# Softmax denominators from two partial sums: four key chunks added on GpSimd, two on VectorE, joined by the ones matmuls of TensorE

## The chip, the cores and the metric

The kernel runs on one core of one Trainium2 chip. Times are device microseconds (us) of one execution, so smaller is better. TensorE (PE in the profile; PEld is its weight load), VectorE (DVE), ScalarE (ACT), GpSimd (POOL) and SyncE (SP) are its engines. The program gives each its own instruction list, and the views of the profile name which engine waited for which.

## The reference, cut to what matters

```python
# q, k, v: (4, 8, 768, 64); 16 clusters for each head
q_assign = argmax(einsum('bhsd,hcd->bhsc', q_n, c_n), -1)      # the same for k
mask = q_assign[:, :, :, None] == k_assign[:, :, None, :]
scores = where(mask, scale * q @ k.T, -1e9)
attn = exp(scores - max(scores));  attn = attn / (sum(attn, -1) + 1e-9)
x = (attn @ v)                     # then, for each of 3072 rows of 512:
# a gate picks 2 of 8 rank-16 adapters; out = x + sum of w * (x @ A[e]) @ B[e]
```

The change touches only `sum(attn, -1)`, the denominator of the softmax.

## The kernel before

Two heads form a pair; there are 16 pairs, four for each batch element. A pair's 768 queries are worked off in three thirds of 256, and its 768 keys in six chunks of 128, which lie on the partitions. For each third, TensorE computes the scores, ScalarE takes exp of two chunks at a time into the tile `ET` (keys on partitions, 2 heads x 256 queries in the free dimension), and TensorE multiplies with `v`. The value matmuls of a third are issued three thirds behind its scores. The denominator needs the sum of the six chunks, and then the sum over the 128 partitions, which TensorE does with a matrix of ones:

```python
def add_unit(p, t, u, ready):                     # u: which two chunks have just been through exp
    f = lambda k_: ET[p, t][:, k_].rearrange("p h c -> p (h c)")
    def reduce():                                 # chunks 3, 4, 5 and T, which is GpSimd's sum of 0, 1, 2
        nc.vector.tensor_reduce(SS[p][:, :, t * TQ:(t + 1) * TQ]...,
                                ET[p, t][:, 3:T + 1].rearrange("p k h c -> p h c k"), axis=AX.X, op=ALU.add)
    if u < 2:
        W.op("POOL", 1.3, lambda: nc.gpsimd.tensor_tensor(f(T), f(T if u else 0), f(u + 1), ALU.add), ...)
    else:
        W.after([("add", p, t, 1)], lambda x: W.op("DVE", 2.2, reduce, ...))

def denominators(p):                              # once a pair: "the denominator group"
    ps = misc([128, 384])
    for h in range(2):
        for f in range(2):
            o = 32 * (2 * h + f)
            nc.tensor.matmul(ps[o:o + 32, :], ones[:, 0:32], SS[p][:, h, f * 384:(f + 1) * 384])
    # ... VectorE: transpose, reciprocal, transpose; DMAs spread the result to all rows (rDb)
```

Two more parts play a role. `route(p)` is a group of four TensorE matmuls of the same shape, whose input is the q and k of a later pair, turned by VectorE (`nc.vector.transpose` into `qkT`). And the last pair has a wider form, `denominators_wide`, in two parts.

`W` is a small simulator that runs while the program is built; it only decides in which order the instructions are put into each engine's list. Numbers such as 1.3 and 2.2 in it are its guesses of durations.

The softmax here doesn't subtract the row's maximum and nothing guards it: scores larger than these inputs give would overflow.

## Time and profile before

| kernel before | |
|---|---|
| time, median of 4 runs | 364.99 us (364.70 to 365.08) |
| the profiled execution | 367.25 us, a span of 365.5 on the core |
| TensorE, VectorE, ScalarE, GpSimd busy | 88%, 81%, 56%, 50% |
| TensorE and VectorE busy from 100 to 300 us, of 200 | 187.2 and 182.1 us |
| granted TensorE clock | 0.963 in the profiled execution |

The profiled execution is 2 us slower than the median of the timed runs. Among all 33 runs of this kernel the times lie between 364.5 and 368.0. In the 29 of them with a listed clock it lies between 0.961 and 0.972. So a difference of two single profiles is good to some 3 us only; times are compared by their runs.

The costliest groups that matter here: line, engine, operation, out<-in, shapes, count | busy us in total, mean ns of one | idle time of the engine just before them and what ended it.

```profile
L433 DVE TENSOR_REDUCE SS<-ET 128x512 f32<-128x2048 f32 x48 | 182.6, 3804 | 14.7 <-ACT ET L422 9.6
L437 POOL TENSOR_TENSOR ET<-ET 128x512 f32<-128x512 f32 x96 | 122.6, 1277 | 71.7 <-ACT ET L422 68.6
...
L298 DVE STREAM_TRANSPOSE qkT<-qk_pc 128x768 f32<-128x768 f32 x28 | 26.9, 961 | 0.0
L449 PE MATMUL ps<-SS,ones 128*32 128x384 f32 x120 | 22.6, 514 | 3.7 <-DVE SS L433 3.7
```

The reductions alone are 182.6 of VectorE's 296.5 us. A float32 matmul shows as two records, so 120 records are 60 matmuls, four for each of 15 pairs. The view of TensorE's own waits (who waited for whom: total us, how often, longest):

```profile
PE sc L419 <- ACT ET L422: 9.7, 23, 0.7
PE ps L321 <- DVE qkT L298: 7.7, 7, 2.8
...
PE ps L449 <- DVE SS L433: 3.7, 4, 2.3
PE ps L484 <- DVE SS L433: 3.4, 1, 3.4
...
PE ps L321 <- ACT ET L422: 2.2, 2, 1.1
```

L419 are scores, L321 routing, L449 the denominator group, L484 the wide one. This view counts only time in which no matmul is recorded as running; its lines for the start and for the tail's adapter work, which the change leaves as they are, are left out.

```profile
54.01 0.85 PE L321 MATMUL ps<-qkT,cnP 128*32 128x384 f32 x8 [2.83 <-DVE qkT L298]
54.79 4.50 PE L510 MATMUL o_180<-ET,v_nat 128*64 128x256 f32 x24
59.22 0.75 PE L419 MATMUL sc<-Q_1_145,K_1_147 80*128 80x256 f32 x4
59.80 0.64 PE L419 MATMUL sc<-Q_0_144,K_0_146 80*128 80x256 f32 x4
61.17 0.74 PE L419 MATMUL sc<-Q_0_144,K_0_146 80*128 80x256 f32 x4 [0.73 <-ACT ET L422]
61.84 0.83 PE L449 MATMUL ps<-SS,ones 128*32 128x384 f32 x2
65.03 1.43 PE L449 MATMUL ps<-SS,ones 128*32 128x384 f32 x6 [2.35 <-DVE SS L433]
```

The routing group waits 2.83 us for VectorE. Then the 24 records of value matmuls take 4.50 us; elsewhere in this trace the same 24 take 2.81. The denominator group starts at 61.84, stops for the last third's sum, and ends at 66.46: 4.62 us for work that takes 0.85 when its inputs are there. Of the 3.8 us too many, only 2.35 are listed as idle time. The granted clock was halved from 54.9 to 58.3 us and from 65.1 to 68.6, just after each of the two waits (the clock column of the windows view).

### The profile page before, as it was taken

The numbers are of one execution on the slowest core, as the hardware profiler recorded it, in microseconds if no ns is written. First come the engines' busy times: TensorE is split into PE (matmuls) and PEld (weight loads), VectorE is DVE, ScalarE is ACT, GpSimd is POOL, SyncE is SP. The second block draws the span as 40 slices with busy tenths as digits, with TensorE's granted clock in tenths as the row PEclk, the third lists the DMA queues.
The fourth block names the chain that finished last, engine by engine and source line by source line (L and its number), as shares of the span: only waits on it lengthen the run. The fifth ranks groups of instructions, "written<-read, shape, count | busy, mean of one in ns | idle before, by whom it ended". The sixth has DMA issues, their size and how long they took to land.

```text
span 365.5 us, 6465 instructions
## 1 busy us (share of the span) xinstructions
PE 320.4 (88%) x2432; PEld 206.3 (56%) x2444; DVE 296.5 (81%) x324; ACT 204.6 (56%) x233; POOL 184.1 (50%) x211
## 2 busy tenths in 40 slices
PE   4789957899898998898989989898989999996964
PEld 1466544555555565566666655566656557673533
DVE  6328697898989898989798998989897989898052
ACT  3267574374756646658576484665757547471213
POOL 5243737466665645564738347465565464551000
PEclk9758998899999999999999999999999999998999
DMA  7820536154725333535556441717365102020204
GB/s 159 179 43 2 118 72 112 39 87 95 130 72 93 77 64 50 119 56 136 125 124 142 94 75 24 142 30 174 79 164 131 30 12 70 18 82 29 84 4 172
DMA packets 111695, 32.07 MB, mean 88 GB/s; under 512 B 101488, under 2 KB 107504, under 8 KB 111664
## 3 DMA queue, kind: packets, MB, share of 16 engines
q1 hardware_dynamic: 111664, 31.66, 40.3%
q8 instruction: 19, 0.31, 0.4%
q14 instruction: 12, 0.10, 0.1%
HBM read 19.45 MB, written 6.29 MB: 70 GB/s over the span
## 4 chain that ended last, share of the span: by engine, by line
PE 52%; DVE 22%; ACT 8%; issue 6%; SPq 5%; DMA 5%; POOL 0%; DVEq 0%; ACTq 0%
PE o_179 L510 15%; PE o_180 L510 12%; PE sc L419 12%; DVE SS L433 9%; ACT ET L422 7%; PE ps L449 5%; DMA rDb<-rDb 3%; DVE qkT L298 3%; PE ps L321 3%; DVE rDb L460 2%; SPq L472 2%; SPq L154 2%; DVE xT L524 1%; SPq L165 1%; DVE d_t L455 1%
## 5 line engine op out<-in xcount | busy, mean ns | idle before, releaser
L422 ACT ACTIVATE ET<-sc,expbias 128x1024 f32<-128x1024 f32 x144 | 154.5, 1118 | 114.1 <-PE sc L419 113.9
L433 DVE TENSOR_REDUCE SS<-ET 128x512 f32<-128x2048 f32 x48 | 182.6, 3804 | 14.7 <-ACT ET L422 9.6
L437 POOL TENSOR_TENSOR ET<-ET 128x512 f32<-128x512 f32 x96 | 122.6, 1277 | 71.7 <-ACT ET L422 68.6
L510 PE MATMUL o_180<-ET,v_nat 128*64 128x256 f32 x576 | 70.4, 395 | 0.0
L510 PE MATMUL o_179<-ET,v_nat 128*64 128x256 f32 x576 | 68.5, 388 | 0.0
L527 POOL CAST xTb<-xT 128x256 bf16<-128x256 f32 x48 | 18.7, 399 | 81.6 <-DVE xT L524 81.4
L419 PE MATMUL sc<-Q_0_144,K_0_146 80*128 80x256 f32 (+1 forms) x288 | 54.5, 319 | 5.1 <-ACT ET L422 4.6
L419 PE MATMUL sc<-Q_1_145,K_1_147 80*128 80x256 f32 (+1 forms) x288 | 53.3, 309 | 5.7 <-ACT ET L422 5.1
L510 PEld LDWEIGHTS o_180<-ET,v_nat 128*64 128x64 f32 x576 | 40.8, 141 | 27.5 <-issue 6.6
L419 PEld LDWEIGHTS sc<-Q_0_144,K_0_146 80*128 80x128 f32 (+1 forms) x288 | 41.9, 203 | 21.4 <-issue 11.8
L510 PEld LDWEIGHTS o_179<-ET,v_nat 128*64 128x64 f32 x576 | 39.7, 138 | 24.4 <-issue 4.6
L419 PEld LDWEIGHTS sc<-Q_1_145,K_1_147 80*128 80x128 f32 (+1 forms) x288 | 39.6, 190 | 21.6 <-issue 11.1
L298 DVE STREAM_TRANSPOSE qkT<-qk_pc 128x768 f32<-128x768 f32 x28 | 26.9, 961 | 0.0
L449 PE MATMUL ps<-SS,ones 128*32 128x384 f32 x120 | 22.6, 514 | 3.7 <-DVE SS L433 3.7
L321 PE MATMUL ps<-qkT,cnP 128*32 128x384 f32 x128 | 14.3, 518 | 12.2 <-DVE qkT L298 7.7
L274 ACT COPY ot<-ps 128x512 f32<-128x512 f32 x23 | 13.4, 582 | 16.4 <-issue 9.0
L455 DVE STREAM_TRANSPOSE d_t<-ps 128x384 f32<-128x384 f32 x15 | 8.7, 583 | 14.9 <-PE ps L449 14.9
L460 DVE STREAM_TRANSPOSE rDb<-r_pk 128x384 f32<-128x384 f32 x30 | 15.6, 557 | 0.5
L664 PE MATMUL ps<-ident_f,xT 128*128 128x128 f32 x96 | 14.6, 275 | 0.5 <-DVE gt L653 0.4
L449 PEld LDWEIGHTS ps<-SS,ones 128*32 128x32 f32 x120 | 4.3, 108 | 16.4 <-DVE SS L433 10.9
L357 ACT ACTIVATE ohs<-ps,mscale 128x768 f32<-128x768 bf16 x15 | 13.4, 896 | 0.0
L524 DVE TENSOR_TENSOR xT<-o_179,rDb 128x256 f32<-128x256 f32 x24 | 9.6, 400 | 3.1 <-PE o_179 L510 3.1
(151 smaller groups left out, 241.0 us busy)
## 6 DMA issues: line engine op xcount, KB each, us to landing
v_nat<-in_v_dram SPq DMA_DIRECT2D x16, 384.0 KB, 3.8
out_dram<-ot SPq DMA_DIRECT2D x24, 256.0 KB, 2.3
qk_pc<-in_k_dram SPq DMA_DIRECT2D x56, 96.0 KB, 3.5
qk_pc<-in_q_dram SPq DMA_DIRECT2D x56, 96.0 KB, 3.1
rDb<-rDb SPq DMA_DIRECT2D x60, 48.0 KB, 1.9
qk_nat<-in_q_dram SPq DMA_DIRECT2D x4, 192.0 KB, 4.0
qk_nat<-in_k_dram SPq DMA_DIRECT2D x4, 192.0 KB, 4.2
K_1_147<-ohs SPq DMA_DIRECT2D x16, 48.0 KB, 2.1
```

The costliest lines, as they stand in the source:

```text
L274: W.op(eng, n / 1200 + 0.19, lambda: nc.scalar.copy(dst(), src), key=key, then=then)
L298: "DVE", 0.9, lambda: nc.vector.transpose(qkT[p][:, w * S:(w + 1) * S], qk_pc[p][:, w].rearrange("p n d -> p (n d)")),
L321: nc.tensor.matmul(ps[o:o + 32, :].rearrange("p (m c) -> p m c", m=3), cnP[:, j, :], xv[:, w, f])
L419: nc.tensor.matmul(ps[:, i, h, :], kd[0:rows, h, kc * 128:(kc + 1) * 128].bitcast(F32R), qd[0:rows, h, t * TQ:(t + 1) * TQ].bitcast(F32R))
L422: W.op("ACT", 1.12, lambda: nc.scalar.activation(ET[p, t][:, 2 * u:2 * u + 2].rearrange("p a h c -> p (a h c)"), ps[:].rearrange("p a h c ...
L433: nc.vector.tensor_reduce(SS[p][:, :, t * TQ:(t + 1) * TQ].rearrange("p h c -> p h c"), ET[p, t][:, 3:T + 1].rearrange("p k h c -> p h c k ...
L437: W.op("POOL", 1.3, lambda: nc.gpsimd.tensor_tensor(f(T), f(T if u else 0), f(u + 1), ALU.add), ready, key=key)
L449: nc.tensor.matmul(ps[o:o + 32, :], ones[:, 0:32], SS[p][:, h, f * 384:(f + 1) * 384])
L460: nc.vector.transpose(rb[:, f * 384:(f + 1) * 384].rearrange("p (a b) -> p a b", b=32), r_pk[:].unsqueeze(2).to_broadcast([128, 12, 32]))
L510: nc.tensor.matmul(oab[i % 2][64 * h:64 * h + 64, i // 2 % 2, :], v_nat[p][:, h, kc * D:(kc + 1) * D], ET[p, t][:, kc, h, :], start=(kc == ...
L527: "POOL", 0.65, lambda: nc.gpsimd.tensor_copy(xTb[p][:, a:b], xT[p][:, a:b]), y, key=("xb", i))))
L664: nc.tensor.matmul(ps[:, dc * 128:(dc + 1) * 128], xT[NP * b + dc][:, t * 128:(t + 1) * 128], ident_f[:], is_transpose=True, start=(dc == ...
```

## The change

Its intent: take most of the summing from VectorE. GpSimd adds chunks 0 to 3 (three adds in place of two), VectorE adds only chunks 4 and 5 (one two-input add in place of the four-chunk reduction), and the two sums are never added to each other: TensorE multiplies the ones with both and accumulates.

```diff
-            ET[p, t] = etp.tile([128, T + 1, 2, TQ], F32, name="ET")
+            ET[p, t] = etp.tile([128, T, 2, TQ], F32, name="ET")
             if t == 0:
-                SS[p] = wk2.tile([128, 2, S], F32, name="SS")
+                SS[p] = wk2.tile([128, 2, 2, S], F32, name="SS")
...
+        e = lambda k_: ET[p, t][:, k_]
+        a, b = (SS[p][:, i, :, t * TQ:(t + 1) * TQ] for i in range(2))
+        add = lambda x_, k_: W.op("POOL", 1.3, lambda: nc.gpsimd.tensor_tensor(a, x_, e(k_), ALU.add), ready, key=key)
-        if u < 2:
-            W.op("POOL", 1.3, lambda: nc.gpsimd.tensor_tensor(f(T), f(T if u else 0), f(u + 1), ALU.add), ready, key=key)
+        if u == 0:
+            add(e(0), 1)
+        elif u == 1:
+            add(a, 2)
+            add(a, 3)
         else:
-            W.after([("add", p, t, 1)], lambda x: W.op("DVE", 2.2, reduce, max(x, ready), key=("ss", p, t)))
+            W.op("DVE", 0.7, lambda: nc.vector.tensor_tensor(b, e(4), e(5), ALU.add), ready, key=key)
+            W.after([("add", p, t, 1), key], lambda x: W.t.__setitem__(("ss", p, t), x))
...
-        for h in range(2):
-            for f in range(2):
-                o = 32 * (2 * h + f)
-                nc.tensor.matmul(ps[o:o + 32, :], ones[:, 0:32], SS[p][:, h, f * 384:(f + 1) * 384])
+        for i in range(2):
+            for h in range(2):
+                for f in range(2):
+                    o = 32 * (2 * h + f)
+                    nc.tensor.matmul(ps[o:o + 32, :], ones[:, 0:32], SS[p][:, i, h, f * 384:(f + 1) * 384],
+                                     start=(i == 0), stop=(i == 1))
... (the same in denominators_wide)
```

More of the change, by code (lines that the diff above doesn't have):

```diff
@@ L428, in add_unit @@
     def add_unit(p, t, u, ready):
-        f = lambda k_: ET[p, t][:, k_].rearrange("p h c -> p (h c)")
-        def reduce():
-            nc.vector.tensor_reduce(SS[p][:, :, t * TQ:(t + 1) * TQ].rearrange("p h c -> p h c"),
-                                    ET[p, t][:, 3:T + 1].rearrange("p k h c -> p h c k"), axis=AX.X, op=ALU.add)
+        e = lambda k_: ET[p, t][:, k_]
+        a, b = (SS[p][:, i, :, t * TQ:(t + 1) * TQ] for i in range(2))
         key = ("add", p, t, u)
-        if u < 2:
-            W.op("POOL", 1.3, lambda: nc.gpsimd.tensor_tensor(f(T), f(T if u else 0), f(u + 1), ALU.add), ready, key=key)
-        else:
-            W.after([("add", p, t, 1)], lambda x: W.op("DVE", 2.2, reduce, max(x, ready), key=("ss", p, t)))
+        add = lambda x_, k_: W.op("POOL", 1.3, lambda: nc.gpsimd.tensor_tensor(a, x_, e(k_), ALU.add), ready, key=key)
[4 more added lines that the diff above has]
+            add(a, 3)
+        else:
+            W.op("DVE", 0.7, lambda: nc.vector.tensor_tensor(b, e(4), e(5), ALU.add), ready, key=key)
+            W.after([("add", p, t, 1), key], lambda x: W.t.__setitem__(("ss", p, t), x))
     rDb = {}
@@ L482, in denominators_wide @@
         ps = misc([128, n])
-        for h in range(2):
-            nc.tensor.matmul(ps[64 * h:64 * h + 64, :], ones[:], SS[p][:, h, a:a + n])
+        for j in range(2):
+            for h in range(2):
+                nc.tensor.matmul(ps[64 * h:64 * h + 64, :], ones[:], SS[p][:, j, h, a:a + n],
+                                 start=(j == 0), stop=(j == 1))
         def inverse():
```

## The prediction

> **What bounds it now.** The page's busy table: TensorE 320.4 us (88% of 365.5), VectorE 296.5, ScalarE 204.6, GpSimd 184.1. Between 100 and 300 us the windows view shows TensorE busy 37.4 to 38.0 of every 40 us, VectorE 36.2 to 36.6. TensorE sets the pace; VectorE, nearly as full, makes it wait. The waits view, TensorE alone: score matmuls for the exp 9.7 us; routing matmuls for the transposed q/k 7.7; denominator matmuls for the sums 3.7, and once 3.4 at the tail. Another hides in the denominator group: on the chain it takes 1.33 us, but 0.85 where its inputs are there, as the routing group of the same shape (four 128x384 float32 matmuls into four 32-row groups) does: about 5.5 us over the run.
>
> **What the change does.**
> - VectorE: 48 reductions of 3.80 us (182.6) become 48 adds, 128x512 float32. The Trainium skill, "VectorE: DVE Perf Modes", errata section, gives (N+151)/0.96 ns = 691 ns; the trace agrees at another size (128x384 one-hot op 558 ns, formula 557). The skill, "SBUF — State Buffer", section "Who interferes with whom": a VectorE op with two SBUF inputs and a GpSimd op that reads SBUF exclude each other; a reduction never contends. No run here shows it. I expect adds of 0.7 to 2 us, mean 1.1; VectorE falls to about 170 us.
> - GpSimd: 96 adds of 1.28 us become 144: +61 us, plus up to 33 us blocked by VectorE's adds: 245 to 280 us. Per pair of heads (19.5 us) about 15.4 us of work plus 2 blocked: it fits. A pair's last sums are needed some 8 us after their exp; GpSimd needs 2.6.
> - TensorE: the order is the same but for added matmuls. Each of 15 denominator groups gets four more, side by side: two passes of 384 columns, 0.64 us (0.85 less a fixed 0.2; estimate). 15 x 0.64 = 9.6 us, all on the critical path. The last pair's wide group grows by 1.3 us.
>
> **Sum.** Recoverable: 7.7 + 3.7 + 5.5 = 17 us of waits for VectorE. Paid: about 10. Net -7. Tail: the last sums were done at 335.1 us; now an add of 0.7 follows the last exp (331.4), but the wide group is longer: the next value matmuls start 2.7 us earlier. Total -10 us: most of VectorE's 130 us buys nothing, as it lay under TensorE's work.
>
> **Predicted: 355 us (80%: 349 to 361); faster by over 2% 0.72, within 0.25, slower 0.03.**
>
> **What would show each step.** Groups: VectorE adds' shortest near 0.69 us; GpSimd adds x144, mean above 1.28 with a tail near 2; the denominator group 1.4 to 1.6 us on the chain, no wait for sums before it. Waits: TensorE for the transposed q/k under 2 us, for the sums under 1, for the exp unchanged or a little up (two score buffers and the 1.12 us exp fix it). Windows 100 to 300: TensorE 38 or more of 40, VectorE about 20. Chain: VectorE's share from 22% to under 12%.
>
> **What would make it wrong.** (a) The lock costs more: GpSimd falls behind in the stage with three roundings (7.6 us of work in a 6.4 us slot) and the denominator group waits for it: 360 or more. (b) The added ones matmuls don't run four abreast: +1.5 us a group, no gain. (c) The routing waits were for the reciprocals' DMA and the q/k loads queued behind it: 3 to 5 us less gain. (d) VectorE's lateness hid more inside TensorE's modelled durations: 348.

## More of the kernel before

The page's first table and its clock row, in tenths of full speed over 40 slices of the span:

```profile
PE 320.4 (88%) x2432; PEld 206.3 (56%) x2444; DVE 296.5 (81%) x324; ACT 204.6 (56%) x233; POOL 184.1 (50%) x211
...
PEclk9758998899999999999999999999999999998999
```

## The result, and the profile after

The changed kernel takes 346.25 us, the median of 4 runs (345.05 to 347.17), against 364.99 for the kernel before on the same chip. The ratio is 0.9486, with a 95% interval of 0.945 to 0.9522: faster by 5.1%, or 18.7 us by the medians. Every ratio here is the mean time of one kernel's fast runs over that of the other's of the same rounds, so it is not quite the ratio of the medians that are quoted. The direction was predicted, the size was not: 10 us were forecast, and 346.25 lies below the range of 349 to 361.

The same lines as before, first the page's table and clock row:

```profile
PE 312.4 (91%) x2572; PEld 201.5 (59%) x2572; DVE 170.4 (50%) x324; ACT 203.9 (59%) x233; POOL 262.3 (76%) x259
...
PEclk9899999999999999999999999999999999999999
```

TensorE did more matmuls and was still busy for 8 us less in all. That is possible only if the recorded busy time before contained waiting or slow running. The groups:

```profile
L433 POOL TENSOR_TENSOR SS<-SS,ET 128x512 f32<-128x512 f32 x96 | 127.0, 1323 | 7.0
L433 POOL TENSOR_TENSOR SS<-ET 128x512 f32<-128x512 f32 x48 | 63.2, 1318 | 31.4 <-ACT ET L422 31.3
...
L440 DVE TENSOR_TENSOR SS<-ET 128x512 f32<-128x512 f32 x48 | 45.0, 938 | 23.9 <-ACT ET L422 23.9
...
L452 PE MATMUL ps<-SS,ones 128*32 128x384 f32 x240 | 22.5, 492 | 0.0
```

The 240 denominator records of after take 22.5 us, and the 120 of before took 22.6. The waits of TensorE, with the same lines left out. The wait for the transposed q/k is down from 7.7 to 0.2 us, and both lines for the sums are gone:

```profile
PE sc L419 <- ACT ET L422: 11.2, 26, 0.7
...
PE sc L419 <- DMA Q_1_145<-ohs: 0.9, 3, 0.4
PE o_180 L516 <- DVE xT L530: 0.6, 1, 0.6
```

And TensorE's timeline in the second pair of heads:

```profile
47.34 0.85 PE L321 MATMUL ps<-qkT,cnP 128*32 128x384 f32 x8
48.81 2.81 PE L516 MATMUL o_180<-ET,v_nat 128*64 128x256 f32 x24 [0.62 <-DVE xT L530]
...
54.19 1.50 PE L452 MATMUL ps<-SS,ones 128*32 128x384 f32 x16
```

The value matmuls are back at 2.81 us, and the denominator group, now with twice the matmuls, takes 1.50 us without a break.

**A ruler.** The end of the denominator group of each pair is a good milestone, as it stands at the same place in TensorE's list in all kernels. (A rival to rule out first: the simulator `W` could have put the instructions in another order. In the traces, the order of TensorE's operations is the same before and after, but for the added matmuls and a dozen small matmul records that are missing from the trace of before, and ScalarE's differs in one place.) From the timelines (us; "ordinary 12" are the pairs after the second, up to the last group but one):

| | start to 1st end | second pair | ordinary 12 | last of the 15 | tail | span |
|---|---|---|---|---|---|---|
| before | 45.5 | 20.9 | 234.8 | 17.5 | 46.7 | 365.5 |
| after | 41.6 | 14.1 | 227.0 | 18.1 | 42.9 | 343.7 |

The first three ordinary pairs fell from 18.8 to 18.3 us each, the three whose denominator group stands beside work of the adapter gates from 20.9 to 20.3, the rest from 19.2 to 19.4 down to 18.4 to 18.8. The second pair fell from 20.9 to 14.1. The first column is a warning: 3.9 us of the 21.8 between these two profiles lie in the first 45 us, in which TensorE's list differs by four matmuls, and where the granted clock differs much (0.61 against 0.92 in the mean from 10 to 32 us).

### The profile page after: what moved, and what is told of

It is laid out like the page before. It is cut to its first block, busy times and chain, and to the rows that moved or that the text cites. A ratio compares the mean times of both kernels' runs of the same rounds, so it can differ in the third digit from the quotient of the medians.

```text
span 343.7 us, 6753 instructions
## 1 busy us (share of the span) xinstructions
PE 312.4 (91%) x2572; PEld 201.5 (59%) x2572; DVE 170.4 (50%) x324; ACT 203.9 (59%) x233; POOL 262.3 (76%) x259
## 3 DMA queue, kind: packets, MB, share of 16 engines
q1 hardware_dynamic: 111664, 31.66, 43.2%
## 4 chain that ended last, share of the span: by engine, by line
PE 76%; ACT 11%; DVE 6%; DMA 2%; issue 2%; SPq 2%; POOL 0%; DVEq 0%; ACTq 0%; POOLq 0%
PE o_179 L516 19%; PE sc L419 19%; PE o_180 L516 16%; ACT ET L422 9%; PE ps L452 6%; PE ps L321 4%; PE ps L670 2%; PE ps L542 2%; DMA Q_1_145<-ohs 1%; PE ps L289 1%; PE ps L203 1%; PE ps L673 1%; ACT ohs L357 1%; DVE ident_b L188 1%; PE ps L348 1%
## 5 line engine op out<-in xcount | busy, mean ns | idle before, releaser
L433 POOL TENSOR_TENSOR SS<-SS,ET 128x512 f32<-128x512 f32 x96 | 127.0, 1323 | 7.0
L433 POOL TENSOR_TENSOR SS<-ET 128x512 f32<-128x512 f32 x48 | 63.2, 1318 | 31.4 <-ACT ET L422 31.3
L516 PE MATMUL o_180<-ET,v_nat 128*64 128x256 f32 x576 | 67.6, 383 | 0.6 <-DVE xT L530 0.6
L516 PE MATMUL o_179<-ET,v_nat 128*64 128x256 f32 x576 | 67.5, 383 | 0.0
L419 PE MATMUL sc<-Q_1_145,K_1_147 80*128 80x256 f32 (+1 forms) x288 | 53.3, 309 | 6.3 <-ACT ET L422 4.9
L419 PE MATMUL sc<-Q_0_144,K_0_146 80*128 80x256 f32 (+1 forms) x288 | 51.7, 306 | 6.4 <-ACT ET L422 6.3
L440 DVE TENSOR_TENSOR SS<-ET 128x512 f32<-128x512 f32 x48 | 45.0, 938 | 23.9 <-ACT ET L422 23.9
L516 PEld LDWEIGHTS o_180<-ET,v_nat 128*64 128x64 f32 x576 | 39.2, 137 | 26.8 <-issue 4.7
L516 PEld LDWEIGHTS o_179<-ET,v_nat 128*64 128x64 f32 x576 | 39.2, 137 | 23.7 <-issue 4.1
L419 PEld LDWEIGHTS sc<-Q_1_145,K_1_147 80*128 80x128 f32 (+1 forms) x288 | 39.5, 190 | 22.5 <-issue 12.9
L419 PEld LDWEIGHTS sc<-Q_0_144,K_0_146 80*128 80x128 f32 (+1 forms) x288 | 39.2, 190 | 21.7 <-ACT ET L422 10.7
L533 POOL CAST xTb<-xT 128x256 bf16<-128x256 f32 x48 | 27.2, 578 | 18.2 <-DVE xT L530 18.2
L530 DVE TENSOR_TENSOR xT<-o_180,rDb 128x256 f32<-128x256 f32 x24 | 9.9, 413 | 30.4 <-PE o_180 L516 26.2
L452 PE MATMUL ps<-SS,ones 128*32 128x384 f32 x240 | 22.5, 492 | 0.0
L530 DVE TENSOR_TENSOR xT<-o_179,rDb 128x256 f32<-128x256 f32 x24 | 9.9, 413 | 21.2 <-PE o_179 L516 14.9
```

The source lines that it names most:

```text
L419: nc.tensor.matmul(ps[:, i, h, :], kd[0:rows, h, kc * 128:(kc + 1) * 128].bitcast(F32R), qd[0:rows, h, t * TQ:(t + 1) * TQ].bitcast(F32R))
L433: add = lambda x_, k_: W.op("POOL", 1.3, lambda: nc.gpsimd.tensor_tensor(a, x_, e(k_), ALU.add), ready, key=key)
L440: W.op("DVE", 0.7, lambda: nc.vector.tensor_tensor(b, e(4), e(5), ALU.add), ready, key=key)
L452: nc.tensor.matmul(ps[o:o + 32, :], ones[:, 0:32], SS[p][:, i, h, f * 384:(f + 1) * 384], start=(i == 0), stop=(i == 1))
L516: nc.tensor.matmul(oab[i % 2][64 * h:64 * h + 64, i // 2 % 2, :], v_nat[p][:, h, kc * D:(kc + 1) * D], ET[p, t][:, kc, h, :], start=(kc == ...
L530: nc.vector.tensor_tensor(xT[p][:, a:b], oab[i % 2][:, i // 2 % 2], rDb[p][:, a:b], ALU.mult)
```

## The experiments

The theory, after the result: (A) what made TensorE lose time was VectorE's lateness, in open waits, in waits inside groups, and in a halved clock after the long ones; the added matmuls are a price that is paid in full. Its rivals: (B) the added matmuls fill time that TensorE would wait anyway, or a chain from GpSimd to VectorE to TensorE is what counts; (C) the gain is a luckier clock at the start, or earlier DMA; (D) the slow stretches have another cause than waits. In what follows, "before" in a ratio means the kernel before in the same rounds on the same chip.

### The added matmuls left out (wrong result)

```diff
-        for i in range(2):
+        for i in range(1):
...
-                                     start=(i == 0), stop=(i == 1))
+                                     start=(i == 0), stop=(i == 0))
```

> Wrong result on purpose: the changed kernel without the second set of ones matmuls. Theory A (the added matmuls lie wholly on TensorE's critical path; in the changed kernel's chain a group takes 1.43 us against 0.85, the wide group 2.7 against 1.6): 15 x 0.58 + 1.1 = 9.8 us less than the changed kernel, 336 us (333 to 339). Rival B (they fill time in which TensorE waits anyway, for the exp above all): 342 us or more.

Measured: 338.7 us (336.47 to 339.35), ratio 0.9249 (0.9206 to 0.9292). The changed kernel has 0.9486 and, in a second set of rounds, 0.9499; the difference of 0.024 to 0.025 is about 9 us (of 365). In the ruler, the first ordinary pairs take 17.7 us against 18.3, and the group 0.85 against 1.50. Theory A holds on the price: some 9 us, give or take 2 by the intervals, where 9.8 was expected. So VectorE's lateness was worth about 18 + 9 = 27 us, not the 21 (17 and 4 at the tail) of the prediction.

### VectorE's load put back, without its old work

```diff
         else:
-            W.op("DVE", 0.7, lambda: nc.vector.tensor_tensor(b, e(4), e(5), ALU.add), ready, key=key)
+            def add2():
+                nc.vector.tensor_reduce(b..., ET[p, t][:, 3:T].rearrange("p k h c -> p h c k"), ...)   # overwritten
+                nc.vector.tensor_tensor(b, e(4), e(5), ALU.add)
+            W.op("DVE", 2.2, add2, ready, key=key)
```

> Correct result: the changed kernel with a useless reduction of three chunks on VectorE ahead of each of its adds (about 2.9 us, overwritten), so that VectorE is as full as before and only the work that it is freed from is put back. Theory A (the gain is VectorE's lateness, in waits and in the half clock that follows them): all of the gain is lost and the added matmuls remain: 368 to 376 us, with TensorE waits for transposed q/k and sums back. Rival C (the gain is a luckier clock at the start, or earlier DMA): under 355 us.

Measured: correct, 365.91 us (364.16 to 367.21), ratio 1.000 (0.9955 to 1.0046). All of the gain is gone, and the waits are back (3.3 us came once for an output):

```profile
PE ps L321 <- DVE qkT L298: 6.5, 6, 2.8
...
PE ps L456 <- DVE SS L443: 2.2, 4, 0.8
```

The time missed the 368 to 376 of theory A from below. VectorE came out less full than before: the useless reductions took 1.91 us each in place of the 2.9 expected, so that VectorE was busy for 278 us and not 297. That this is why the time stayed lower fits, but was not tested. Rival C (under 355) is out as the main cause.

### VectorE's reduction made cheaper, and nothing else (wrong result)

```diff
-            nc.vector.tensor_reduce(SS[p]..., ET[p, t][:, 3:T + 1].rearrange("p k h c -> p h c k"), axis=AX.X, op=ALU.add)
+            for k0 in (3, 5):
+                nc.vector.tensor_reduce(SS[p]..., ET[p, t][:, k0:k0 + 2].rearrange("p k h c -> p h c k"), axis=AX.X, op=ALU.add)
```

> Wrong result on purpose: the kernel before, with VectorE's four-chunk reduction (3.80 us) replaced by two two-chunk reductions into the same output, the second overwriting the first. The same elements are read; nothing moves to another engine and TensorE adds nothing. Theory A (VectorE's time alone makes TensorE wait): the pair takes about 2.5 us (two of 1.24, as the reduction in place of the changed kernel's add took), VectorE falls from 81% to about 68% busy, and most of the waits go: 340 to 347 us. Rival B (the gain came from moving a chunk to GpSimd, or from the sums being done earlier by splitting them): 357 or more.

Measured: 339.47 us (338.46 to 340.26), ratio 0.9262 (0.9203 to 0.932). It reads the same elements, on the same engine, and leaves GpSimd and TensorE as they were; the order of all operations in the trace, with two reductions for one, is that of before. The groups view of this kernel:

```profile
L434 DVE TENSOR_REDUCE SS<-ET 128x512 f32<-128x1024 f32 x96 | 119.0, 1239 | 22.5 <-ACT ET L422 17.6
```

Two reductions of 1.24 us read what one of 3.80 read before. VectorE at 70% busy in place of 81% is enough to bring TensorE to within a microsecond of the kernel without the added matmuls. This is the cleanest evidence for theory A: the gain is VectorE's time, and moving a chunk to GpSimd only serves to shorten it. VectorE's busy time fell by 59 us (296.5 to 237.7), and that bought what the change bought, before its price, with 126 (296.5 to 170.4).

### The clock held up in before's two long waits

```diff
         ps = misc([128, 384])
+        if p == 3:                                 # in route; the same with p == 1 in denominators
+            for _ in range(14):
+                nc.tensor.matmul(ps[:], ident_b[:], wdummy[:, 0:384])
```

> Correct result: the kernel before, with 14 dummy matmuls of 384 columns ahead of the routing matmuls and of the denominator matmuls of the two places where TensorE waited longest (2.8 us at 51 us, 2.4 us at 63 us in the trace of before), into the same PSUM tile, overwritten. They shorten no wait. Theory A (TensorE's clock was halved after these two waits: granted 0.67 and 0.66 in the stretches after them, and a value group took 4.43 us in place of 2.74): about 3 us faster than before, 362 us, both stretches at clock 1.0. Rival D (the slow stretches have another cause): the same as before, 365, or slower.

Measured: correct, 363.14 us (362.17 to 365.35), ratio 0.9936 (0.9889 to 0.9983): 2 us rather than 3. The interval leaves out 1. TensorE's timeline in the second pair (L319 are the dummies):

```profile
47.16 2.45 PE L319 MATMUL ps<-wdummy,ident_b 128*128 128x384 bf16 x14
50.20 0.85 PE L324 MATMUL ps<-qkT,cnP 128*32 128x384 f32 x8 [0.59 <-DVE qkT L298]
50.98 2.81 PE L516 MATMUL o<-ET,v_nat 128*64 128x256 f32 x24
```

The routing group still waits for VectorE, but the value matmuls after it take 2.81 us and not 4.50, and the second pair takes 18.7 us in the ruler, not 20.9. From 46 to 72 us the granted clock is 1.00 here and 0.87 in before. The Trainium skill, "TensorE: Matmul & The Clock Gate", section "HAM oscillation", describes this: a gap in matmul activity makes the clock gate fall back to half clock (it gives gaps of more than about 3.4 us; the recorded gaps here were shorter, see the last section). Rival D is out for these stretches.

### The clock held up everywhere in before

The same dummies, and 5, 3 and 7 more ahead of three groups in the first 22 us, and 24 ahead of the last wide group.

> Correct result: the kernel before with dummy matmuls in all its long TensorE waits: at the start (5, 3 and 7 of them), the two waits of the second pair (14 each) and the wait for the last sums (24). No wait is shortened. Theory A (halved clock after waits is a part of its own of what before loses: up to 4 us in the first 45 us, 2 in the second pair, 1 at the tail): 358 to 361 us, with a smaller spread than before's and clock 0.99 or more. Rival D (clock matters only with luck at the start): 363 or more.

Measured: correct, 362.73 us (361.96 to 363.18), ratio 0.9901 (0.9861 to 0.9942), clock 0.991 to 0.995. The level lies above the 358 to 361 of theory A: holding up the clock everywhere was worth about 3 us of the median (with an interval that leaves out 1), hardly more than the two waits alone (the dummies at the start cost something too: the first group ends at 42.1 us in this profile, and at 41.7 in a profile of the former run with its clock up by luck). The spread shrank to 1.2 us, as expected.

### The start of the changed kernel held up

> Correct result: the changed kernel with the same dummy matmuls at the start (5, 3 and 7) as the hot form of before, none elsewhere. Theory A (the changed kernel's spread of 345 to 349 us is the length of the halved clock in the first 30 us, and it has no long TensorE wait after that): 345 us (343.5 to 346), spread under 1.5 us, clock 0.99 or more; against the hot form of before (362.7) the change is then worth about 17.5 us with the clock taken out. Rival: spread as before, so it has another source.

Measured: correct, 347.02 us (346.54 to 347.64), ratio 0.9476. The spread is 1.1 us, as theory A had it, but the level is not 345: the first group ends at 42.5 us in its profile, against 41.6 and 43.2 in the two profiles without dummies, so they delay the start about as much as they save. Against the hot form of before (the run just above) the changed kernel stands at 0.9476 / 0.9901 = 0.957, about 16 us. So with the clock taken out on both sides, about 16 of the 18 to 19 us remain; by the two intervals, 14 to 18. Rival C explains some 3 us, and hardly more than 5.

The changed kernel as it is was run once more as a reference:

> The changed kernel as it is, as the reference for the runs beside it on this chip: 345 to 347.5 us, the spread coming from how long the halved clock lasts in the first 30 us.

It took 347.89 us (347.02 to 348.9), ratio 0.9499 (0.9456 to 0.9543): just above the range expected, and the same ratio within the intervals.

### Does VectorE's add block GpSimd?

VectorE's two-chunk sum by a one-input reduction:

```diff
-            W.op("DVE", 0.7, lambda: nc.vector.tensor_tensor(b, e(4), e(5), ALU.add), ready, key=key)
+            W.op("DVE", 1.9, lambda: nc.vector.tensor_reduce(b..., ET[p, t][:, 4:T].rearrange("p k h c -> p h c k"), ...
```

> Correct result: the changed kernel with VectorE's two-chunk sum done by a reduction (one input) in place of a two-input add. Theory L (VectorE's add, with both inputs in SBUF, and GpSimd's reads shut each other out): the reduction takes a steady 1.9 us (spread under 0.2), GpSimd's adds fall from a mean of 1.32 us to 1.28 with none over 1.35, its casts of the output from 0.58 to 0.40 us; the time stays within 3 us of the changed kernel, as both engines have room. Rival M (GpSimd's adds are longer because of their new output or their own crowding): its means stay at 1.32 and 0.58.

Measured: correct, 348.54 us (347.21 to 350.12), ratio 0.9518 (0.9466 to 0.957), within the noise of the changed kernel. The views of GpSimd's adds (shortest/median/longest ns), first of the changed kernel, then of this one:

```profile
L433 POOL TENSOR_TENSOR SS<-SS,ET x96: 1267/1282/1691, 24.6 to 312.3; 128x512 f32<-128x512 f32 x96
L433 POOL TENSOR_TENSOR SS<-ET x48: 1289/1306/1752, 23.2 to 309.5; 128x512 f32<-128x512 f32 x48
```

```profile
L433 POOL TENSOR_TENSOR SS<-SS,ET x96: 1264/1278/1302, 26.7 to 316.9; 128x512 f32<-128x512 f32 x96
L433 POOL TENSOR_TENSOR SS<-ET x48: 1287/1304/1322, 25.3 to 314.2; 128x512 f32<-128x512 f32 x48
```

The long tail is gone, GpSimd's casts of the output fell from a mean of 0.58 to 0.40 us, and VectorE's operation took a steady 1.20 to 1.26 us (1.9 had been expected), where the add had taken 0.65 to 1.71. This agrees with the Trainium skill, "SBUF — State Buffer", section "Who interferes with whom": a VectorE instruction with two inputs in SBUF (the memory of the tiles) and a GpSimd instruction that reads SBUF shut each other out, and a reduction does not take part. But it is worth nothing here, since both engines have room.

### One sum again, by a second add on VectorE

One set of ones matmuls, and VectorE adds its sum to GpSimd's:

```diff
-            W.after([("add", p, t, 1), key], lambda x: W.t.__setitem__(("ss", p, t), x))
+            W.after([("add", p, t, 1), key], lambda x: W.op(
+                "DVE", 0.7, lambda: nc.vector.tensor_tensor(a, a, b, ALU.add), x, key=("ss", p, t)))
```

> Correct result: VectorE also adds its sum to GpSimd's (one more 0.7 to 1 us add a third), so one set of ones matmuls is enough. Theory A: TensorE's saving as without the second set, VectorE has room (50% busy now, about 62% then): 337 us (334 to 340), faster than both kernels. Rival B: VectorE stands in its own order waiting for GpSimd's last add, and hands the waits back to TensorE: 345 us or more, with denominator groups that wait for sums.

Measured: correct, 344.53 us (343.73 to 346.94), ratio 0.9441 (0.9391 to 0.949): a miss of theory A, close to rival B's level. The ruler tells where: its first ordinary pairs take 17.7 us, as fast as without the added matmuls, but the second pair takes 19.5 us in place of 14.1. There TensorE has few value matmuls behind which late work could hide (2.81 us of them, against 8.2 in an ordinary pair). Two waits for VectorE lie in it. The routing group waits first, and half clock follows (50.3 to 53.7 us); then the denominator group waits for the sum. Lines of the timeline:

```profile
48.52 0.85 PE L321 MATMUL ps<-qkT,cnP 128*32 128x384 f32 x8 [1.79 <-DVE qkT L298]
49.98 4.50 PE L517 MATMUL o<-ET,v_nat 128*64 128x256 f32 x24 [0.60 <-DVE xT L531]
...
57.34 2.35 DVE L442 TENSOR_TENSOR SS<-SS 128x512 f32<-128x512 f32 x1
57.89 1.25 POOL L433 TENSOR_TENSOR SS<-ET 128x512 f32<-128x512 f32 x1
...
59.74 0.85 PE L453 MATMUL ps<-SS,ones 128*32 128x384 f32 x6 [1.87 <-DVE SS L442]
```

A 0.7 us add took 2.35 us beside GpSimd's work, and the group took 3.55 us in place of 0.85: 2.7 of the pair's loss. The rest is the routing wait and the 1.7 us of slow value matmuls after it. So rival B's late sum holds in this one pair of the first 15, where it is a little under half of what went wrong, and once more in the last pair (1.8 us before the wide group), not in the others.

### Two sums where TensorE has room, one elsewhere

Two sums for the first two pairs and the last, folded for the other 13; in code, `nset(p)` is 2 or 1 and chooses between the two forms above.

> Correct result: two sums for the first two pairs and the last (there TensorE has room, or the last sum is waited for), folded into one on VectorE for the other 13. Theory A (the folded kernel lost its gain only in the second pair of heads, where TensorE has few value matmuls to hide VectorE's wait for GpSimd: 19.5 us between denominator groups against 14.1, and then half clock; its later pairs ran 17.7 us against 18.3): 13 x 0.6 = 8 us less than the changed kernel, 338 us (336 to 341). Rival B (VectorE's waiting costs in every pair): 344 or more.

Measured: correct, 340.6 us (337.92 to 343.17 over all four; the slowest counts as slow, and the ratio is of the others), ratio 0.9263 (0.9193 to 0.9333). The second pair is back at 14.1 us, and the folded ones take 17.7 to 19.7, as in the folded kernel, but for the first two of them (18.4 and 18.5). With the dummies at the start:

> Correct result: the kernel that folds the sums for 13 of 16 pairs, with the dummy matmuls at the start. Theory A (clock at the start independent of the sums): 340.6 less about 2: 338 us (336.5 to 339.5) and a spread under 1.5 us, the fastest of all kernels tried.

Measured: correct, 341.21 us (340.86 to 341.38), ratio 0.9311. The spread is 0.5 us; the level is no better, as with the changed kernel, and the hoped-for 338 was missed.

### One chunk more on GpSimd, and a three-chunk reduction

The runs had shown that three-chunk reductions take 1.9 us where four-chunk ones take 3.8. So the smallest change to the kernel before:

```diff
-                                    ET[p, t][:, 3:T + 1].rearrange("p k h c -> p h c k"), axis=AX.X, op=ALU.add)
+                                    ET[p, t][:, 4:T + 1].rearrange("p k h c -> p h c k"), axis=AX.X, op=ALU.add)
...
-        if u < 2:
-            W.op("POOL", 1.3, lambda: nc.gpsimd.tensor_tensor(f(T), f(T if u else 0), f(u + 1), ALU.add), ready, key=key)
+        add = lambda i, k_: W.op("POOL", 1.3, lambda: nc.gpsimd.tensor_tensor(f(T), f(i), f(k_), ALU.add), ready, key=key)
+        if u == 0:
+            add(0, 1)
+        elif u == 1:
+            add(T, 2)
+            add(T, 3)
```

> Correct result: the kernel before, with only one chunk more added on GpSimd, and VectorE's reduction over three chunks (GpSimd's sum and two more) in place of four. One sum, no added matmuls, no two-input op on VectorE. Three-chunk reductions took 1.9 us in the run with the useless reduction, four-chunk ones 3.8 in before. Theory A (what counts is VectorE's time and TensorE's added matmuls): VectorE has 48 x 1.9 = 91 us less, TensorE pays nothing: 338 us in the pairs that follow the second, the second pair may wait for GpSimd as in the folded run: 338 to 343 us, GpSimd's adds a steady 1.28 us. Rival B (the sum of GpSimd and VectorE in turn is late in every pair): 346 or more.

Measured: correct, 339.07 us (338.47 to 339.78), ratio 0.9254 (0.9225 to 0.9284). The intervals of this and of the changed kernel (0.945 at the least) do not meet, so it beats both kernels. (In its trace four of VectorE's transpositions of q/k stand at another place in VectorE's order than before, so the edit is not quite alone.) Its two groups:

```profile
L433 DVE TENSOR_REDUCE SS<-ET 128x512 f32<-128x1536 f32 x48 | 91.6, 1909 | 24.2 <-POOL ET L436 11.3 <-ACT ET L422 11.1 <-POOL xTb L531 1.5
...
L436 POOL TENSOR_TENSOR ET<-ET 128x512 f32<-128x512 f32 x144 | 183.6, 1277 | 47.1 <-ACT ET L422 40.2
```

TensorE pays nothing, GpSimd's adds are a steady 1.28 us, and the ruler reads 42.5, 15.0, 218.8, 16.9 and 44.8 us.

## Why the prediction was right or wrong

- **"TensorE sets the pace; VectorE, nearly as full, makes it wait"**: right. Cheaper reductions alone gave 339.47 us; a useless load on VectorE took the whole gain back (365.91).
- **VectorE's add 0.7 to 2 us, mean 1.1; VectorE about 170 us; GpSimd 245 to 280**: right: mean 0.94 us, 170.4 and 262.3 us. The shortest add took 0.65 us. The exclusion of the two engines is real and costs nothing here.
- **GpSimd stays off the critical path**: right. In the changed kernel TensorE's waits show no sum at all.
- **What would show each step**: as forecast. From 100 to 300 us TensorE is busy 193.9 of 200 us and VectorE 102.4; VectorE's share of the page's chain (the work that ended last, followed back step by step to what released it) fell from 22% to 6%, and TensorE's rose from 52% to 76%.
- **The price, "about 10" and 1.3 at the tail**: about right, a little dear. Leaving the matmuls out saved some 9 us by the ratios. An ordinary pair takes 0.6 us more with them (18.3 against 17.7), and 0.64 was estimated.
- **"Recoverable: 7.7 + 3.7 + 5.5 = 17 us"**: this is the step that failed, by size and not by kind. With the tail it came to 21 us, and about 27 were there. The ruler can be split along TensorE's timeline. From the end of the first denominator group to the end of the fifteenth, before takes 273.3 us and the kernel without the added matmuls 249.4. The 23.9 us between them lie in three places, and small differences elsewhere come to -0.5; the tail adds 3.5 us (46.7 against 43.2):
  - 12.9 us in 14 denominator groups. Over all 15, before spends 26.2 us from their first to their last matmul, and the other kernel 15 x 0.85 = 12.75: 13.5 us, where the prediction had 3.7 + 5.5 = 9.2. Its 5.5 fits the 11 groups without recorded idle time (1.37 to 1.42 us each, 5.9 above 0.85). The other four were counted by their recorded idle time alone, 3.7 us; but the group of the second pair took 4.62 us and the three beside the adapter gates 2.11 to 2.13, in all 7.6 above 4 x 0.85.
  - 9.8 us in and before the routing groups, where the prediction had 7.7. Another 2.2 us of their waits stood in the waits view under the exp; they went too.
  - 1.6 us of value matmuls at half clock, where the prediction has no term. After a wait of 2.8 us they ran 4.50 us in place of 2.81. Holding the clock in the two long waits was worth 2 us, in all long waits about 3, of which a part at the start is not the change's doing.
- **"What would make it wrong", point (d), "VectorE's lateness hid more inside TensorE's modelled durations: 348"**: this is the larger part of what happened, in the four groups. It was named and given too little weight; the half clock was not named. Points (a), (b) and (c) did not happen: no group waited for GpSimd, the added matmuls ran abreast, and the waits for q/k went from 7.7 us to 0.2.
- **"Most of VectorE's 130 us buys nothing"**: right: 126 us less work (296.5 to 170.4) bought about 27 us of TensorE's time, and 9 of it were spent again. With the two cheaper reductions, a fall of 59 us bought the same 27.
- What stays open: before never had a clock above 0.972 in the 29 runs that list it, while the changed kernel had 0.98 to 0.995. By these clocks, before ran some 20 to 29 us of each execution at half clock, the changed kernel 3 to 14. In the profile of before, 10 us of it follow the two waits and the wait at the tail, and 17 lie at the start (13.9 to 31.0 us); the changed kernel has 3.4 at the start in one profile and 10.2 in the other. Why the start differs so from run to run, and was the slower one in before, is not settled. And why a four-chunk reduction costs twice a three-chunk one was measured, not explained.

## What to carry to other kernels

When one engine sets the pace and another is nearly as full, time the pacing engine from milestone to milestone, not by its recorded idle time: waits in the middle of a group, and slow running after a long wait, were booked as work here. Before work is split over three engines, look at the unit cost of the operation that is too slow: here the four-chunk reduction was dear (3.80 us against 1.91 for three chunks), and one chunk fewer in it beat the split that cost TensorE 9 us. Late work hurts most where the pacing engine has little else to do (the folded kernel's sum was late for TensorE by over 1 us in the second and the last pair alone), so look at that stage on its own.

## What the Trainium skill lacked or had wrong

- "VectorE: DVE Perf Modes" (perf-mode tier table, rules for authors) gives float32 `tensor_reduce` as 1x and no more. Here, with the reduced chunks 2 KB apart, two chunks took 1.24 us (1024 elements read), three 1.91 us (1536) and four 3.80 us (2048): 1.2 ns an element for the first two and 1.9 for the last. No page has this step.
- The same page's (N+151)/0.96 ns for a float32 two-input add, called exact there, gives 691 ns for 512 elements; nine of the 48 adds took 683 to 694 ns, but nine others 651 to 681.
- "SBUF — State Buffer", "Who interferes with whom": confirmed here. Mean GpSimd add 1.32 us beside two-input adds (longest 1.75), longest 1.32 us beside reductions. It does not say that the loser can wait through more than one instruction: a VectorE add took 2.35 us, 1.66 more than its 0.69, where one GpSimd add takes 1.28. It began at 57.34 us, while a GpSimd cast ran until 57.92 and an add after it until 59.14 (that it waited for both is our reading).
- "TensorE: Matmul & The Clock Gate" names an idle window of about 3.4 us for the fall to half clock. Here a recorded idle time of 2.83 us, and one of 2.35 us, were enough: 24 value records took 4.50 us in place of 2.81 after the first. In the folded kernel 1.79 us, 0.85 of work and 0.60 more of idle time were enough too, while 1.87 us in one piece there, and 1.67 in the kernel with cheaper reductions, were not followed by half clock. So the length of one idle time does not decide it.
- No page says that dummy matmuls which hold the clock can cost as much as they save: at the start of the changed kernel they cut the spread from 2.1 to 1.1 us and did not lower the time (347.02 against 346.25 and 347.89).
